# Two-level fast matrix products on one Trainium2 core: four PSUM banks for the forks, and another order of products and evictions in the steady unit

## Chip, cores and metric

The kernel runs on one core of one Trainium2 chip. The metric is the device time of one execution in microseconds (us), lower is better.

## The reference

A cross network of six layers on 16384 rows of 1024 columns in bfloat16:

```python
x = x0
for l in range(6):
    proj = jnp.einsum('bd,de->be', x, ws[l]) + bs[l]
    x = x0 * proj + x
```

## The kernel before

The kernel takes 1024 rows at a time through the six layers. One layer of one such block is a **unit**, and there are 96. A product of 2 by 2 blocks is made with seven products instead of eight (P1 to P7). In a **steady unit** (89 of 96) two of the seven, P5 and P2, are again made of seven inner products each (`5p1` to `5p7`, `2p1` to `2p7`). An outer product has four column blocks m = 0 to 3, each four matmuls of 128x128 by 128x512; an inner product is four matmuls with 256 columns.

PSUM has eight banks here: `pA[0..3]` for the outer sums, `pX[0..3]` for inner products and forks. A **fork** is a ScalarE copy of a sum from one bank to another, so that the sum goes on in both. F.m copies P1+P6 from `pA[m]` to a `pX` bank, where P3 is added; P7 and P4 go on in `pA[m]`:

```python
for m in range(KH):
    xb = m if one else m % 2
    group(f"P6.{m}", "6", pA[m], A[m], T[2], ["T2", A[m]], m, False)
    copy(f"F.{m}", pX[xb][:], pA[m][:], [A[m]], [Xn[xb]])
    group(f"P3.{m}", "3", pX[xb], Xn[xb], B22, [XI[1, 1], Xn[xb]], m, False)
    biased(f"E3.{m}", U[:, m, :], pX[xb][:], 0, m, [Xn[xb]], [f"U.{m}"])
    group(f"P7.{m}", "7", pA[m], A[m], T[3], ["T3", A[m]], m, False)
    ...
```

The inner products have forks of their own. This is the part that the argument touches (X is 5 with banks a, b = 0, 1, or 2 with banks 2, 3):

```python
inner(6, a, False)
copy(X + "f2", pX[b][:], pX[a][:], [Xn[a]], [Xn[b]])      # 2f2
inner(3, b, False)
copy(X + "e_c12", iu[X][:, 0], v3(b), [Xn[b]], [X + "u0"])
inner(7, a, False)                                        # 2p7 waits for 2f2
copy(X + "e_u3", iu[X][:, 1], v3(a), [Xn[a]], [X + "u1"])
inner(4, a, False)
copy(X + "e_c21", c(1, 0), v3(a), [Xn[a]], cn(1, 0))
ttop(X + "cc", ...)                                       # VectorE, needs both iu halves
```

`E1.m`, `E3.m` and so on are ScalarE evictions. VectorE makes the differences T1 to T4 that feed P5, P6, P7 and P4, and the layer's update. Five of its steps come up below: `5cc` and `2cc` add up inner results that ScalarE has put into `iu`, Q1 needs all of product 2's results, `2e_c21` among them, Qa ends that part of the update, and Ua needs the evictions E3. Each operation has a rank ("name@time"), and every engine's order is by rank, data allowing. `R2` is the table for all steady units but the first two, 87 units.

Of the kernel before, what the change touches and what calls it, by code (L numbers as in the profile page):

```python
# [24 lines left out]

R2 = ranks("""
P1.0@0 P1.2@0.86 5p5@1.73 5p1@2.16 P1.3@2.6 2p1@3.46 5p2@3.9 5p6@4.34 2p5@4.78 P1.1@5.21 5p7@6.08 5p3@6.51 2p2@6.95
2p6@7.39 5p4@7.82 P6.0@8.26 P6.1@9.13 2p7@9.99 2p3@10.43 P3.0@10.86 2p4@11.73 P6.2@12.16 P3.1@13.03 P6.3@13.89
P3.2@14.75 P3.3@15.62 P7.1@16.48 P7.0@17.34 P7.2@18.21 P7.3@19.07 P4.1@19.93 P4.0@20.8 P4.2@21.66 P4.3@22.52
E1.0@1.07 5e_p5@2.38 5f1@3.03 E1.2@3.48 5e_c11@4.55 5f2@5.2 2e_p5@5.65 2f1@6.3 5e_u3@6.75 E1.3@7.23 E1.1@7.8  # L30
2e_c11@8.37 5e_c21@8.85 2f2@9.33 F.0@9.78 5e_c12@10.23 2e_u3@10.71 2e_c12@11.18 F.1@11.66 E3.0@12.11 2e_c21@12.68
F.2@13.23 E3.1@14.1 F.3@14.96 E3.2@15.82 E3.3@16.69 E7.0@18.41 E7.1@18.98 E7.2@19.55 E7.3@20.14 E4.0@21.87 E4.1@22.44
E4.2@23.01 E4.3@23.59
T1@-1.14 5t13@0.59 5t2@3.06 2t13@3.39 5t4@5.13 2t2@6.6 T2@6.93 2t4@8.07 T4@8.4 5cc@10.88 T3@11.48 2cc@12.61 Q1@13.35
Qm@14.62 Qa@15.89 Ua@17.43 Um@18.7 Ux@19.97 Va@21.11 Wma@23.38 Wmb@24.58 Wx@25.31 Vm@27.38 Vx@28.85
""")
R0 = ranks("""
# [111 lines left out]
def kernel(  # L149
# [121 lines left out]
    for u, (pr, l) in enumerate(units):  # L271
        one, first, last = level1(u), u == 0, u == NU - 1
# [13 lines left out]
        def group(name, w, bank, bname, rhs, rname, m, start, u=u):  # L286
            def fn():
                for k in range(KH):
                    nc.tensor.matmul(bank[:], lhsT=wt[(u, w)][:, k, m * P:(m + 1) * P], rhs=rhs[:, k, :],  # L289
                                     start=(start and k == 0), stop=(k == KH - 1), skip_group_check=True)  # L290
            add(name, fn, rname + [f"w{u}.{w}" + ("a" if name in ("P5.0", "P5.1") and u == 0 else "")] if pr == 0 else rname, [bname], [w])

        def copy(name, dst, src, rd, wr):
            add(name, lambda: nc.scalar.copy(out=dst, in_=src), rd, wr)  # L294

        def biased(name, dst, src, eh, m, rd, wr, l=l):
            c = l * KD + eh * KH + m
            add(name, lambda: nc.scalar.activation(out=dst, in_=src, func=IDENT, bias=b_all[:, c:c + 1], scale=1.0), rd, wr)  # L298
# [52 lines left out]
        if first:  # L351

            for i, (d, n) in enumerate(TURNED):
                for k in range(KH):
                    xb = k if i < 2 else 2 + k % 2
# [75 lines left out]
                     ip5[X][:].unsqueeze(1).to_broadcast([P, 2, KQ, NQ]), ADD, [X + "u0", X + "u1", X + "ps"],  # L431
                     cn(0, 1) + cn(1, 1))
        for m in range(KH):
            xb = m if one else m % 2
            group(f"P6.{m}", "6", pA[m], A[m], T[2], ["T2", A[m]], m, False)
            copy(f"F.{m}", pX[xb][:], pA[m][:], [A[m]], [Xn[xb]])
            group(f"P3.{m}", "3", pX[xb], Xn[xb], B22, [XI[1, 1], Xn[xb]], m, False)
            biased(f"E3.{m}", U[:, m, :], pX[xb][:], 0, m, [Xn[xb]], [f"U.{m}"])
            group(f"P7.{m}", "7", pA[m], A[m], T[3], ["T3", A[m]], m, False)
            biased(f"E7.{m}", V[:, m, :], pA[m][:], 1, m, [A[m]], [f"V.{m}"])  # L440
            group(f"P4.{m}", "4", pA[m], A[m], T[4], ["T4", A[m]], m, False)
            if not (last and m == KH - 1):
                biased(f"E4.{m}", W[:, m, :], pA[m][:], 1, m, [A[m]], [f"W.{m}"])
# [201 lines left out]
```

## Time and profile before

| | before |
|---|---|
| median of 3 runs | 2277.09 us |
| span of the profiled run, granted clock | 2275.3 us, 0.999 |
| TensorE busy, matmul records | 2267.7 us, 12993 |
| VectorE, ScalarE busy | 92%, 81% |
| one steady unit, from recurring blocks | 23.45 us |

The lines behind these are in the prediction. The busy share of TensorE is no measure of holes below 0.16 us: a 512-column matmul is recorded as 379 ns, while the next one starts 216 ns later. So I use **starts**. A *hole* below is the time by which the start of the next matmul is later than 216 ns (512 columns) or 109 ns (256 columns) after the one before. "Holes in all" is the sum of those over 6 ns between 208 and 2200 us of a trace; for before it is 7.26 us.

### The profile page before, as it was taken

Reading aid. Unit: us, or ns where it says so; the run is one execution under the profiler, and the core shown is the slowest. Engines: PE = TensorE matmul, PEld = TensorE weight load, DVE = VectorE, ACT = ScalarE, POOL = GpSimd, SP = SyncE. Lnnn points to the kernel's source line nnn. Section 1 sums busy time; section 2 is a strip of 40 time slices with the busy share of each in tenths; the row PEclk is TensorE's granted clock in tenths of the full one; section 3 lists DMA queues with packets and bytes.
Section 4 is the critical chain, followed back from the end, with each engine's and each line's share of the span. In section 5 each row is a group of like instructions: output and inputs, shape, how many; then the busy total and the mean of one; then the engine's idle time right before and its main releaser. Section 6 shows DMA issues by size and latency. Waiting matters only on the chain.

```text
span 2275.3 us, 35076 instructions
## 1 busy us (share of the span) xinstructions
PE 2267.7 (100%) x12993; PEld 1266.7 (56%) x12993; DVE 2084.0 (92%) x2331; ACT 1844.5 (81%) x3234; POOL 24.5 (1%) x46
## 2 busy tenths in 40 slices
PE   9999999999999999999999999999999999999998
PEld 4455555555555555555555555555555555555554
DVE  8999999999999999999999999999999999989997
ACT  6678888888888888888888888888888888888887
POOL 1110000000000000000000000000000000000000
PEclk9999999999999999999999999999999999999999
DMA  8779797796977969779697796977969689696872
GB/s 280 231 269 297 252 249 262 221 297 210 246 264 222 286 216 255 257 220 286 213 269 247 227 283 205 283 235 227 286 200 286 232 230 286 196 291 227 234 248 66
DMA packets 620493, 557.03 MB, mean 245 GB/s; under 512 B 391456, under 2 KB 546592, under 8 KB 620320
## 3 DMA queue, kind: packets, MB, share of 16 engines
q1 hardware_dynamic: 614240, 534.58, 79.0%
q0 software_dynamic: 5488, 19.93, 2.3%
q8 instruction: 102, 1.67, 0.3%
q14 instruction: 71, 0.58, 0.1%
q10 hardware_dynamic: 592, 0.27, 0.0%
HBM read 437.79 MB, written 52.43 MB: 215 GB/s over the span
## 4 chain that ended last, share of the span: by engine, by line
PE 99%; DMA 0%; ACT 0%; DVE 0%; issue 0%
PE pA L289 58%; PE pX L411 24%; PE pX L289 17%; DMA ev<-in_x_dram 0%; PE pX L359 0%; PE pA L505 0%; PE pX L505 0%; DVE x0T L516 0%; ACT x0T L363 0%; ACT pX L294 0%; PE pA L366 0%
## 5 line engine op out<-in xcount | busy, mean ns | idle before, releaser
L289 PEld LDWEIGHTS <-wp 128*128 128x128 bf16 x7904 | 772.5, 98 | 839.5 <-issue 1.6
L289 PE MATMUL pA<-T,wp 128*128 128x512 bf16 x4608 | 1055.1, 379 | 0.0
L298 ACT ACTIVATE ev<-pA,b_all 128x512 bf16<-128x512 f32 x1123 | 705.0, 691 | 211.2 <-PE pA L289 210.8
L411 PEld LDWEIGHTS <-wp 128*128 128x128 bf16 x4984 | 487.0, 98 | 157.3 <-issue 15.4
L202 DVE TENSOR_TENSOR ev<-ev,x0T 128x2048 bf16<-128x2048 bf16 (+2 forms) x483 | 482.9, 1002 | 8.1 <-ACT ev L298 1.5
L202 DVE TENSOR_TENSOR xst<-ev,xst 128x2048 bf16<-128x2048 bf16 x319 | 389.1, 1220 | 19.1 <-DVE ev L202 0.9
L411 PE MATMUL pX<-ti,wp 128*128 128x256 bf16 x2848 | 397.6, 272 | 0.0
L202 DVE TENSOR_TENSOR ev<-ev,ev 128x2048 bf16<-128x2048 bf16 (+1 forms) x283 | 343.9, 1215 | 25.7 <-ACT ev L298 7.6
L289 PE MATMUL pX<-xst,wp 128*128 128x512 bf16 x1376 | 336.3, 379 | 0.0
L298 ACT ACTIVATE ev<-pX,b_all 128x512 bf16<-128x512 f32 x412 | 289.4, 706 | 56.1 <-PE pX L289 46.5
L289 PE MATMUL pA<-xst,wp 128*128 128x512 bf16 x1280 | 313.5, 379 | 0.0
L294 ACT COPY pX<-pA 128x512 f32<-128x512 f32 x412 | 256.2, 625 | 39.1 <-PE pA L289 38.4
L294 ACT CAST ev<-pX 128x512 bf16<-128x512 f32 x384 | 225.2, 620 | 47.8 <-ACT ev L298 37.3
L202 DVE TENSOR_TENSOR ev<-iu,ip 128x1024 bf16<-128x1024 bf16 x178 | 122.6, 689 | 121.1 <-ACT iu L294 121.1
L294 ACT COPY pX<-pX 128x512 f32<-128x512 f32 x356 | 208.7, 587 | 8.7 <-ACT ev L294 0.2
L294 ACT CAST iu<-pX 128x512 bf16<-128x512 f32 x356 | 197.0, 640 | 0.0
L202 DVE TENSOR_TENSOR T<-xst 128x2048 bf16<-128x2048 bf16 x160 | 194.9, 1218 | 0.3
L202 DVE TENSOR_TENSOR T<-xst,T 128x2048 bf16<-128x2048 bf16 x160 | 195.0, 1219 | 0.2
L411 PE MATMUL pX<-T,wp 128*128 128x256 bf16 x1068 | 160.2, 273 | 0.0
L294 ACT CAST ip<-pX 128x512 bf16<-128x512 f32 x178 | 104.8, 589 | 54.0 <-PE pX L411 54.0
L411 PE MATMUL pX<-xst,wp 128*128 128x256 bf16 x888 | 133.2, 273 | 0.0
L202 DVE TENSOR_TENSOR xst<-ev,x0T 128x2048 bf16<-128x2048 bf16 x64 | 78.3, 1223 | 1.6
(50 smaller groups left out, 641.0 us busy)
## 6 DMA issues: line engine op xcount, KB each, us to landing
wp<-Lc SPq DMA_DIRECT2D x538, 512.0 KB, 4.6
wp<-in_ws_dram SPq DMA_DIRECT2D x287, 512.0 KB, 5.4
out_dram<-x0T SPq DMA_DIRECT2D x30, 1024.0 KB, 8.7
Lc<-wp POOLq DMA_DIRECT2D x24, 512.0 KB, 5.9
Lc<-isum POOLq DMA_DIRECT2D x12, 512.0 KB, 6.7
w<-in_ws_dram SPq DMA_DIRECT2D x5, 512.0 KB, 6.3
ev<-in_x_dram SPq DMA_DIRECT2D x3, 512.0 KB, 7.0
out_dram<-x0T SPq DMA_DIRECT2D x3, 256.0 KB, 3.9
```

The source lines that it names most:

```text
L202: nc.vector.tensor_tensor(out=o, in0=a, in1=b, op=op)
L289: nc.tensor.matmul(bank[:], lhsT=wt[(u, w)][:, k, m * P:(m + 1) * P], rhs=rhs[:, k, :], start=(start and k == 0), stop=(k == KH - 1), skip ...
L294: add(name, lambda: nc.scalar.copy(out=dst, in_=src), rd, wr)
L298: add(name, lambda: nc.scalar.activation(out=dst, in_=src, func=IDENT, bias=b_all[:, c:c + 1], scale=1.0), rd, wr)
L411: nc.tensor.matmul(pX[bank][:, m * NQ:(m + 1) * NQ], lhsT=wv[:, k, m * P:(m + 1) * P], rhs=rhs[:, k, :], start=(start and m == 0 and k == ...
```

## The change

The intent: let P6 run ahead of P3 without sharing banks, and close waits in the steady unit. On TensorE P6.3 goes ahead of P3.1. On ScalarE 2e_c11 goes ahead of E1.1, 2f2 ahead of 5e_c21, 2e_c21 ahead of E3.0 and F.3 ahead of E3.1. On VectorE T3 goes ahead of 5cc. The order changes are in `R2` alone; the banks change in all 89 steady units.

```diff
-... P6.2@12.16 P3.1@13.03 P6.3@13.89
+... P6.2@12.16 P6.3@13.03 P3.1@13.89
-... E1.3@7.23 E1.1@7.8
-2e_c11@8.37 5e_c21@8.85 2f2@9.33 F.0@9.78 5e_c12@10.23 2e_u3@10.71 2e_c12@11.18 F.1@11.66 E3.0@12.11 2e_c21@12.68
-F.2@13.23 E3.1@14.1 F.3@14.96 E3.2@15.82 ...
+... E1.3@7.23 2e_c11@7.8 E1.1@8.28
+2f2@8.85 5e_c21@9.33 F.0@9.81 5e_c12@10.43 2e_u3@10.9 2e_c12@11.38 F.1@11.86 2e_c21@12.37 E3.0@12.85
+F.2@13.45 F.3@14.1 E3.1@14.96 E3.2@15.82 ...
-... T4@8.4 5cc@10.88 T3@11.48 2cc@12.61 ...
+... T4@8.4 T3@9.6 5cc@10.88 2cc@12.61 ...
@@
-            xb = m if one else m % 2
+            xb = m
```

More of the change, by code (lines that the diff above doesn't have):

```diff
@@ L27 @@
 P1.0@0 P1.2@0.86 5p5@1.73 5p1@2.16 P1.3@2.6 2p1@3.46 5p2@3.9 5p6@4.34 2p5@4.78 P1.1@5.21 5p7@6.08 5p3@6.51 2p2@6.95
-2p6@7.39 5p4@7.82 P6.0@8.26 P6.1@9.13 2p7@9.99 2p3@10.43 P3.0@10.86 2p4@11.73 P6.2@12.16 P3.1@13.03 P6.3@13.89
+2p6@7.39 5p4@7.82 P6.0@8.26 P6.1@9.13 2p7@9.99 2p3@10.43 P3.0@10.86 2p4@11.73 P6.2@12.16 P6.3@13.03 P3.1@13.89
 P3.2@14.75 P3.3@15.62 P7.1@16.48 P7.0@17.34 P7.2@18.21 P7.3@19.07 P4.1@19.93 P4.0@20.8 P4.2@21.66 P4.3@22.52
-E1.0@1.07 5e_p5@2.38 5f1@3.03 E1.2@3.48 5e_c11@4.55 5f2@5.2 2e_p5@5.65 2f1@6.3 5e_u3@6.75 E1.3@7.23 E1.1@7.8
-2e_c11@8.37 5e_c21@8.85 2f2@9.33 F.0@9.78 5e_c12@10.23 2e_u3@10.71 2e_c12@11.18 F.1@11.66 E3.0@12.11 2e_c21@12.68
-F.2@13.23 E3.1@14.1 F.3@14.96 E3.2@15.82 E3.3@16.69 E7.0@18.41 E7.1@18.98 E7.2@19.55 E7.3@20.14 E4.0@21.87 E4.1@22.44
+E1.0@1.07 5e_p5@2.38 5f1@3.03 E1.2@3.48 5e_c11@4.55 5f2@5.2 2e_p5@5.65 2f1@6.3 5e_u3@6.75 E1.3@7.23 2e_c11@7.8 E1.1@8.28
+2f2@8.85 5e_c21@9.33 F.0@9.81 5e_c12@10.43 2e_u3@10.9 2e_c12@11.38 F.1@11.86 2e_c21@12.37 E3.0@12.85
+F.2@13.45 F.3@14.1 E3.1@14.96 E3.2@15.82 E3.3@16.69 E7.0@18.41 E7.1@18.98 E7.2@19.55 E7.3@20.14 E4.0@21.87 E4.1@22.44
 E4.2@23.01 E4.3@23.59
-T1@-1.14 5t13@0.59 5t2@3.06 2t13@3.39 5t4@5.13 2t2@6.6 T2@6.93 2t4@8.07 T4@8.4 5cc@10.88 T3@11.48 2cc@12.61 Q1@13.35
+T1@-1.14 5t13@0.59 5t2@3.06 2t13@3.39 5t4@5.13 2t2@6.6 T2@6.93 2t4@8.07 T4@8.4 T3@9.6 5cc@10.88 2cc@12.61 Q1@13.35
 Qm@14.62 Qa@15.89 Ua@17.43 Um@18.7 Ux@19.97 Va@21.11 Wma@23.38 Wmb@24.58 Wx@25.31 Vm@27.38 Vx@28.85
```

## The prediction

> **What bounds the kernel now.** I read the page's busy shares first, then its chain that ended last.
>
> ```profile
> PE 2267.7 (100%) x12993; PEld 1266.7 (56%) x12993; DVE 2084.0 (92%) x2331; ACT 1844.5 (81%) x3234; POOL 24.5 (1%) x46
> ...
> PE 99%; DMA 0%; ACT 0%; DVE 0%; issue 0%
> ```
>
> TensorE is busy for the whole span and carries 99% of the chain. The page also gives it a full clock in all 40 slices. The other engines have slack, so the question is only whether TensorE's stream has holes, and the busy share cannot show small ones, because the ends of matmuls are modelled. So I read starts. One steady unit in the chain of waits, from one block of products 7 and 4 to the end of the next products 3:
>
> ```profile
> 1015.79 8.63 PE pA L289 x40
> 1024.42 0.87 PE pX L411 x8
> 1025.30 0.86 PE pA L289 x4
> 1026.16 1.75 PE pX L411 x16
> 1027.91 0.86 PE pA L289 x4
> 1028.77 2.18 PE pX L411 x20
> 1030.95 1.73 PE pA L289 x8
> ```
>
> 40 matmuls of 512 columns in 8.63 us are 215.75 ns each, and 20 of 256 columns in 2.18 us are 109 ns each. A steady unit has five outer products of 16 big matmuls (80) and two times seven inner products of 4 small ones (56): 80 x 0.21575 + 56 x 0.1092 = 17.26 + 6.12 = 23.38 us. The blocks of 40 recur at 992.34 and 1015.79 us in the same view, so a unit takes 23.45 us. Some 0.07 us of a unit is therefore not streaming. The timeline of all engines shows where:
>
> ```profile
> 1030.79 1.89 PE L289 MATMUL pA<-T,wp 128*128 128x512 bf16 x8
> ...
> 1030.95 1.09 ACT L294 CAST ev<-pX 128x512 bf16<-128x512 f32 x2
> 1031.89 0.64 ACT L294 COPY pX<-pX 128x512 f32<-128x512 f32 x1
> ...
> 1032.41 0.60 ACT L294 COPY pX<-pA 128x512 f32<-128x512 f32 x1
> 1032.58 0.60 PE L411 MATMUL pX<-ti,wp 128*128 128x256 bf16 x4
> 1032.58 0.75 PEld L411 LDWEIGHTS <-wp 128*128 128x128 bf16 x7 [0.18 <-issue]
> ```
>
> The first row is P6.0 and P6.1: eight matmuls should take 1.726 us, but the next product (2p7) starts 1.79 us later. The hole is 0.064 us (280 ns between two starts instead of 216 in the trace's own starts). 2p7 adds into pX[2], which the fork 2f2 (the COPY at 1031.89, ending 1032.53) reads; 2p7 starts 0.05 us after that end. So it waits for ScalarE, and the only place where the summary of waits hints at it is the weight loads' row:
>
> ```profile
> L411 PEld LDWEIGHTS <-wp 128*128 128x128 bf16 x4984 | 487.0, 98 | 157.3 <-issue 15.4
> ```
>
> Its "issue 15.4" is 84 pauses of 0.18 us, about one for each of the 87 units that use the changed ranks (96 units less 8 early ones and the last). A second, smaller hole is ahead of P3.3: P3.2 and P3.3 take 1.74 us from 1037.34 to 1039.08, 0.012 us over. P3.3 starts 0.05 us after F.3 (start 1037.60, 0.57 us) ends, and F.3 could only start when P6.3 was done.
>
> **What the skill says.** The Trainium skill, "TensorE: Matmul & The Clock Gate", section on 56 against 53.3 ns, gives N/2.4 GHz plus about 2.5 ns start to start at full clock: 215.7 ns at 512 columns. The trace agrees: 215.75. "Perfetto Trace Analysis", Tensor Engine Instruction, says the end of a matmul is estimated by the profiler; the trace agrees, as it hides the 64 ns hole in a row of busy time. "PSUM — Partial Sum Buffer", PSUM bank collisions, says two engines must not touch one bank at once and waits are to be set by bank; here both holes are a matmul waiting for a ScalarE copy on its bank. The same page, Engine vs sequencer instructions, calls ScalarE's queue strictly first in, first out: moving one eviction ahead delays the ones behind it, and the trace shows ScalarE working back to back from 1028.84 to 1036.5 us.
>
> **The change part by part.** No instruction is added or removed; only order and the banks of forks 2 and 3 change. All waits are reckoned from 2p2's neighbourhood, up to which neither engine's order changes. Durations and distances are from ScalarE's timeline: cast to next 0.475 us, biased eviction to next 0.575, copy to next 0.475 to 0.515; an operation on the bank that the one before it read starts 0.62 after it (5e_p5 at 1024.90, 5f1 at 1025.52); end to a waiting matmul 0.05.
>
> 1. 2e_c11 goes ahead of E1.1, and 2f2 ahead of 5e_c21. Old: E1.3 1029.80, E1.1, 2e_c11, 5e_c21, 2f2 1031.89. New: E1.3 1029.80, 2e_c11 1030.38, E1.1 1030.85, 2f2 1031.42. 2f2 is 0.47 us earlier, ends about 1032.06, and 2p7 is due without a hole at 1032.52: margin 0.4 us. **Gain 0.064 us a unit.**
>
> 2. What pays for it. E1.1 now ends 1031.55 and frees pA[1] at 1031.60; P6.1 is due at 1031.65: margin 0.05. 5e_c21 goes to 1031.93 and is directly followed by F.0 on its bank, so F.0 starts at 1032.58 (0.17 later), ends 1033.15, P3.0 is due at 1033.39: margin about 0.2. Then 5e_c12 1033.06, 2e_u3 1033.54, ending 1034.15 and releasing at 1034.20; 2p4 is due at 1034.26: margin 0.06. Two margins shrink to about 0.05 us; by the sum neither breaks.
>
> 3. P6.3 ahead of P3.1, with four banks. P6.3 now ends 0.86 us earlier; F.3 no longer shares a bank with E3.1 and starts about 1036.63, ending 1037.2, while P3.3 is due at 1038.14: margin 0.9 instead of -0.012. F.2 needs 2e_c21 (now ahead of E3.0, ending 1035.6) and starts near 1036.05 for P3.2 at 1037.27. **Gain 0.012 us a unit.**
>
> 4. T3 ahead of 5cc. VectorE idles 1.44 us at 5cc for ScalarE's iu. T3 (1.22 us) fills that, and Q1 comes some 0.45 us earlier. But Ua waits for E3.3, which is tied to P3.3, and from Ua on the row of VectorE is unchanged up to T2, which ends 1030.65 ahead of P6.0 at 1030.79. Gain on the path: none.
>
> Sum: 0.076 us a unit x 87 = 6.6 us. In the trace's starts, 81 holes of 64 ns and 87 of 12 ns are 6.2 us; a few irregular ones, around 1 us in all, I leave as they are. 2277.1 - 6.2 = 2270.9. I add 0.3 us for a margin that slips now and then: 2271.2.
>
> **Rivals.**
> First, the hole only moves: E1.1 to P6.1, or 2e_u3 to 2p4, becomes the new wait. For it: margins of 0.05 us, and ScalarE's durations spread (592 to 667 ns for iu). Against it: my sums leave both positive. A hole of 20 to 40 ns a unit gives back 2 to 3.5 us: 2273 to 2275.
> Second, ScalarE's later evictions or the new demand for pX[2] and pX[3] hold up products 3, and a unit gets longer than before. For it: forks 2 and 3 must now wait for the inner evictions. Against it: 2e_c21 and 2e_c12 end 0.4 us or more ahead of the forks. It would make 2278 or more.
> Third, weight transfers or the earlier T3 matter: nothing for it, since no TensorE wait on DMA shows in the steady part, and VectorE at 92% is not on the chain. 2277, or my number, unchanged.
>
> **Range and chances.** The floor is the stream without holes: 2277.1 - 6.6 - about 1 = 2269.5. Upwards I allow a new hole of about half the old one. Range 2269.7 to 2275.0. Even all holes together are 0.3% of the time, so faster by 2% is out of reach, and 2% slower would take 0.5 us of new waits a unit, which nothing points to.
>
> **What would show it.** Step 1: the weight loads' "issue" pauses of L411 vanish, and eight P6 matmuls to the next product take 1.73 us. Step 3: the blocks of products 7 and 4 recur every 23.37 to 23.39 us. Step 2: no new hole ahead of P6.1 or 2p4. Step 4: VectorE's idle time at iu falls from 121 us to under 75, with no change of its busy time. It is wrong if a unit still takes 23.43 us or more: then look at those two margins first.

## The result and the profile after

| | before | after |
|---|---|---|
| median of 6 runs | 2277.23 us | 2270.97 us (2270.48 to 2271.21) |
| ratio | | 0.9972, 95% interval 0.9959 to 0.9985 |
| unit, median of the trace's starts | 23.451 us | 23.380 us |
| holes in all | 7.26 us | 0.55 us |

A ratio is the mean time of one kernel's fast runs over that of the other's of the same rounds, so not quite the ratio of the medians. The change is 0.28% faster; its interval is clear of 1.

The page of the kernel after, busy times and the chain that ended last:

```profile
PE 2248.5 (99%) x12754; PEld 1267.4 (56%) x12993; DVE 2092.1 (92%) x2331; ACT 1847.8 (81%) x3234; POOL 24.5 (1%) x46
...
PE 99%; issue 1%; DMA 0%; ACT 0%; SPq 0%; DVE 0%; ACTq 0%
```

TensorE seems to have become idle for 1%, "issue". It has not: there are 12993 weight loads but 12754 matmul records, and each matmul has one weight load. 239 records are missing. The chain of waits of the kernel after shows how that looks:

```profile
1022.09 0.87 PE pX L411 x8
1022.96 0.86 PE pA L289 x4
1023.83 1.75 PE pX L411 x16
1025.57 0.05 issue
1025.62 0.81 PE pA L289 x3
1026.44 2.18 PE pX L411 x20
1028.62 1.73 PE pA L289 x8
1030.35 0.87 PE pX L411 x8
```

"issue" 0.05 and a group of 3 matmuls, 0.81, are together the 0.86 us of a group of four: one record of P1.1 is lost, not the time. I count a gap as a lost record where a weight load stands in it at its usual distance, and as a hole where the loads pause too. The last row is what answers to the prediction: in this stretch the two products behind P6 follow at once. The timeline of the same unit, all engines:

```profile
1028.46 1.89 PE L289 MATMUL pA<-T,wp 128*128 128x512 bf16 x8
1028.51 0.72 ACT L298 ACTIVATE ev<-pA,b_all 128x512 bf16<-128x512 f32 x1
...
1029.09 0.63 ACT L294 COPY pX<-pX 128x512 f32<-128x512 f32 x1
1029.61 0.63 ACT L294 CAST ev<-pX 128x512 bf16<-128x512 f32 x1
...
1030.18 0.60 PE L411 MATMUL pX<-ti,wp 128*128 128x256 bf16 x4
```

P6.0 and P6.1 now take 1030.18 - 1028.46 = 1.72 us until 2p7. The fork 2f2 (COPY) ends at 1029.72, 0.46 us ahead of 2p7. E1.1 (ACTIVATE) ends at 1029.23; P6.1, on the same bank, starts at 1028.46 + 0.863 = 1029.32. In the row of the weight loads the pauses are gone:

```profile
L411 PEld LDWEIGHTS <-wp 128*128 128x128 bf16 x4984 | 487.7, 98 | 151.5 <-issue 0.2
```

And the summary of waits shows where VectorE's idle time went, from 121.1 us at iu before to:

```profile
DVE ev L202 <- ACT iu L294: 60.7, 176, 0.7
...
DVE ev L202 <- ACT ev L298: 46.2, 94, 4.2
```

So the total came out as predicted. Whether each step did is for the experiments.

### The profile page after: what moved, and what is told of

It reads as the page before. It is cut to its first block, busy times and chain, and to the rows that moved or that the text cites. A ratio compares the mean times of both kernels' runs of the same rounds, so it can differ in the third digit from the quotient of the medians.

```text
span 2269.4 us, 34750 instructions
## 1 busy us (share of the span) xinstructions
PE 2248.5 (99%) x12754; PEld 1267.4 (56%) x12993; DVE 2092.1 (92%) x2331; ACT 1847.8 (81%) x3234; POOL 24.5 (1%) x46
## 3 DMA queue, kind: packets, MB, share of 16 engines
q8 instruction: 102, 1.67, 0.3%
## 4 chain that ended last, share of the span: by engine, by line
PE 99%; issue 1%; DMA 0%; ACT 0%; SPq 0%; DVE 0%; ACTq 0%
PE pA L289 58%; PE pX L411 24%; PE pX L289 17%; DMA ev<-in_x_dram 0%; ACT pX L294 0%; PE pA L505 0%; PE pX L359 0%; PE pX L505 0%; DVE x0T L516 0%; ACT ev L294 0%; ACT x0T L363 0%; ACT ip L294 0%; SPq L577 0%; SPq L574 0%; ACTq L294 0%
## 5 line engine op out<-in xcount | busy, mean ns | idle before, releaser
L289 PE MATMUL pA<-T,wp 128*128 128x512 bf16 x4468 | 1033.0, 379 | 7.3
L298 ACT ACTIVATE ev<-pA,b_all 128x512 bf16<-128x512 f32 x1123 | 717.5, 692 | 211.2 <-PE pA L289 164.0
L289 PE MATMUL pX<-xst,wp 128*128 128x512 bf16 x1371 | 323.3, 379 | 0.3
L289 PE MATMUL pA<-xst,wp 128*128 128x512 bf16 x1205 | 302.4, 379 | 3.9
L294 ACT CAST ev<-pX 128x512 bf16<-128x512 f32 x384 | 232.1, 606 | 47.9 <-ACT ev L298 37.4
L294 ACT COPY pX<-pA 128x512 f32<-128x512 f32 x412 | 237.5, 602 | 21.7 <-PE pA L289 18.7
L202 DVE TENSOR_TENSOR ev<-iu,ip 128x1024 bf16<-128x1024 bf16 x178 | 123.2, 692 | 60.7 <-ACT iu L294 60.7
```

What stands on the lines that cost most here:

```text
L202: nc.vector.tensor_tensor(out=o, in0=a, in1=b, op=op)
L289: nc.tensor.matmul(bank[:], lhsT=wt[(u, w)][:, k, m * P:(m + 1) * P], rhs=rhs[:, k, :], start=(start and k == 0), stop=(k == KH - 1), skip ...
L294: add(name, lambda: nc.scalar.copy(out=dst, in_=src), rd, wr)
L298: add(name, lambda: nc.scalar.activation(out=dst, in_=src, func=IDENT, bias=b_all[:, c:c + 1], scale=1.0), rd, wr)
```

## The experiments

"Before" beside a run is the kernel before, in the same rounds.

| run | median us | before beside it | ratio (95%) | holes in all, us |
|---|---|---|---|---|
| e1_scalar_only | 2272.0 | 2276.19 | 0.9982 (0.9969 to 0.9994) | 2.73 |
| e2_pe_and_banks_only | 2275.68 | 2276.19 | 0.9998 (0.9985 to 1.001) | 6.21 |
| e3_t3_only | 2276.58 | 2276.19 | 1.0001 (0.9988 to 1.0015) | 6.77 |
| e4_after_two_banks | 2329.56 | 2276.19 | 1.0234 (1.022 to 1.0248) | 56.8 |
| e5_E11_behind_2f2 | 2320.66 | 2276.79 | 1.0193 (1.0177 to 1.0209) | 48.8 |
| e6_after_T3_back | 2271.8 | 2276.79 | 0.9978 (0.9966 to 0.9991) | 1.67 |
| e7_banks_only | 2275.61 | 2276.79 | 0.9995 (0.9982 to 1.0007) | 5.82 |
| e8_E31_ahead_of_F3 | 2318.9 | 2276.79 | 1.0186 (1.0172 to 1.02) | 47.4 |
| e9_after_again | 2270.5 | 2276.49 | 0.9974 (0.9961 to 0.9986) | 0.56 |
| e10_after_T3_back_again | 2271.46 | 2276.49 | 0.9979 (0.9966 to 0.9991) | 1.72 |
| e11_scalar_and_T3 | 2272.49 | 2276.49 | 0.9982 (0.9969 to 0.9994) | 2.76 |
| e12_only_F3_shares | 2276.4 | 2276.49 | 0.9999 (0.9985 to 1.0013) | 6.57 |

All twelve gave correct results.

### e1: the early ScalarE move alone

```diff
-E1.3@7.23 E1.1@7.8
-2e_c11@8.37 5e_c21@8.85 2f2@9.33 F.0@9.78
+E1.3@7.23 2e_c11@7.8 E1.1@8.28
+2f2@8.85 5e_c21@9.33 F.0@9.78
```

> Kernel before with one move alone: 2e_c11 ahead of E1.1 and 2f2 ahead of 5e_c21 on ScalarE. Theory (the 64 ns hole ahead of 2p7 is a wait for 2f2, and this move alone closes it): unit 23.451 to 23.387 us, the weight loads' 84 pauses of 0.18 us gone, the 12 ns hole ahead of P3.3 stays; 2277.2 - 5.3 = 2271.9 us. Rival (the four banks or the T3 move gave the time): 2277.2, holes as before.

It came to 2272.0 us. No hole is left ahead of 2p7 and the weight loads' pauses fall to 0.5 us: the hole was a wait for 2f2, as predicted. But 5.4 us of holes closed there and the time fell by only 4.2. The starts show why: some 50 holes ahead of P6.0, mostly of about 10 ns and three of 220, and two of 0.13 us ahead of 2p1. Before had three of 160 to 184 ns at P6.0 and none of the small ones. P6.0 waits for T2 from VectorE. The prediction's sum had no such term.

### e2: the rest without the early ScalarE move and T3

```diff
 (kernel after)
-2e_c11@7.8 E1.1@8.28
-2f2@8.85 5e_c21@9.33 F.0@9.81
+E1.1@7.8
+2e_c11@8.37 5e_c21@8.85 2f2@9.33 F.0@9.81
-T3@9.6 5cc@10.88 2cc@12.61
+5cc@10.88 T3@11.48 2cc@12.61
```

> Kernel after with the early ScalarE moves (E1.1, 2e_c11, 5e_c21, 2f2) and T3 put back as before; the four banks, P6.3 ahead of P3.1 and F.3 ahead of E3.1 stay. Theory: the 64 ns hole ahead of 2p7 is back, the 12 ns hole ahead of P3.3 is gone; unit 23.44, 2277.2 - 1.1 = 2276.1 us. Rival (the banks carry the gain): 2271.

The pauses of the weight loads are back (here the same row of this run), the holes ahead of P3.3 are gone, and the unit is 23.442 us as expected:

```profile
L411 PEld LDWEIGHTS <-wp 128*128 128x128 bf16 x4984 | 487.2, 98 | 157.2 <-issue 15.6
```

The time, 0.5 us under before, is not told from zero; the trace's holes fell by 1.05 us.

### e3 and e7: T3 alone, banks alone

```diff
 e3 (kernel before)
-T4@8.4 5cc@10.88 T3@11.48 2cc@12.61
+T4@8.4 T3@9.6 5cc@10.88 2cc@12.61
 e7 (kernel before)
-            xb = m if one else m % 2
+            xb = m
```

> Kernel before with T3 moved ahead of 5cc on VectorE alone. Theory: off the path, VectorE's idle time at iu falls from 121 us to under 75 and appears instead at Ua; unit 23.45, 2277.2 us. Rival (VectorE at 92% also paces): 2275 or less.

> Kernel before with the forks on four banks and no order changed. Theory: F.3 waits for P6.3's end, not for the bank, so nothing moves: the holes of 64 and 12 ns stay, 2277.2 us (within 0.5). Rival (the bank of E3.1 held up F.3): the 12 ns hole closes, 2276.1.

T3 alone did nothing to the time (2276.58 against 2276.19). VectorE's wait at iu fell to 46.5 us; what it saved came back not at Ua, as I expected, but as 76.6 us of waiting for an eviction into `ev`, which by its place in VectorE's row is Q1 waiting for 2e_c21.

Banks alone is a miss. I expected nothing, but all the 12 ns holes ahead of P3.3 are gone, which is the rival's outcome. ScalarE's timeline around F.3, kernel before:

```profile
1036.68 0.69 ACT L298 ACTIVATE ev<-pX,b_all 128x512 bf16<-128x512 f32 x1
1037.60 0.57 ACT L294 COPY pX<-pA 128x512 f32<-128x512 f32 x1 [0.23 <-PE pA L289]
1038.41 0.69 ACT L298 ACTIVATE ev<-pX,b_all 128x512 bf16<-128x512 f32 x1 [0.24 <-PE pX L289]
```

and with four banks alone:

```profile
1036.06 0.69 ACT L298 ACTIVATE ev<-pX,b_all 128x512 bf16<-128x512 f32 x1
1036.92 0.57 ACT L294 COPY pX<-pA 128x512 f32<-128x512 f32 x1 [0.18 <-PE pA L289]
1037.78 0.69 ACT L298 ACTIVATE ev<-pX,b_all 128x512 bf16<-128x512 f32 x1 [0.29 <-PE pX L289]
```

The rows are E3.1, F.3 and E3.2. E3.1 had ended at 1037.37 in the kernel before, 0.23 us ahead of F.3, so its result was not what F.3 waited for. Yet with four banks F.3 is 0.86 us ahead of E3.2 instead of 0.81, 0.05 us earlier. Measured from the start of P6.3's last matmul, F.3 starts 471 ns later in the kernel before and 416 ns later with four banks (medians). In the compiled order F.3 had two waits, one for TensorE and one for ScalarE's own E3.1, and the raw trace has a semaphore instruction at 1037.540, F.3 starting 57 ns after it. With four banks F.3 has the wait for TensorE alone, and no such instruction stands before it.

### e12: only F.3 shares a bank

```diff
 (kernel before)
-            xb = m if one else m % 2
+            xb = m if one else (0, 1, 2, 1)[m]
```

> Kernel before with fork 2 on pX[2] but fork 3 on pX[1], so that F.3 alone shares a bank with E3.1. Theory (F.3 starts about 0.055 us later when it must wait for ScalarE's own E3.1 as well as for TensorE, though E3.1 has long ended): the 12 ns hole ahead of P3.3 is as before, F.3 comes 0.81 us ahead of E3.2 and not 0.86; 2276.5 or so, no faster than 0.6 us under before. Rival (F.2's bank made the hole): the hole is gone, 1.2 us under before.

The 12 to 14 ns holes ahead of P3.3 are back in 85 units, F.3 is again 0.81 us ahead of E3.2 (1037.35 and 1038.16) and 471 ns behind the start of P6.3's last matmul, with the semaphore instruction in front of it, and the time is that of before. So it is F.3's second wait that made this hole. That the extra instruction, and not something else about a second wait, costs the 0.05 us was not tested by itself.

### e4 and e8: what the banks and F.3's place are worth to the new order

```diff
 e4 (kernel after)
-            xb = m
+            xb = m if one else m % 2
 e8 (kernel after)
-F.3@14.1 E3.1@14.96
+E3.1@14.1 F.3@14.96
```

> Kernel after with the forks back on two banks (m mod 2), all orders as after where the data allow. Theory (four banks are what lets P6.3 and F.3 run ahead): F.3 must wait until E3.1 has read pX[1], E3.1 until P3.1 ends; F.3 then ends about 0.6 us past the time P3.3 is due, so a hole of 0.5 to 0.7 us ahead of P3.3 in each of 87 units: 2271 + 45 to 60 = 2316 to 2331 us. Rival (banks are incidental, order counts): within 2 us of 2271.

> Kernel after (four banks, P6.3 ahead of P3.1) with ScalarE's E3.1 put back ahead of F.3. Theory: E3.1 waits for P3.1's end and holds F.3 up in ScalarE's queue; F.3 starts 0.57 us after E3.1, P3.3 waits 0.5 to 0.57 us a unit: 2271 + 43 to 50 = 2314 to 2321 us, a little less than with two banks, where F.3 also waits for E3.1 to end. Rival (only the bank ties F.3 to E3.1): 2271.

Both came out as expected: 2329.56 and 2318.9 us, with one hole ahead of P3.3 in nearly every unit, 0.678 us (e4) and 0.564 us (e8). Here, for e4, TensorE's timeline and then ScalarE's:

```profile
1033.39 1.89 PE L289 MATMUL pX<-x0T,wp 128*128 128x512 bf16 x8
1035.80 1.02 PE L289 MATMUL pX<-x0T,wp 128*128 128x512 bf16 x4 [0.52 <-ACT pX L294]
```

```profile
1034.46 0.69 ACT L298 ACTIVATE ev<-pX,b_all 128x512 bf16<-128x512 f32 x1 [0.65 <-PE pX L289]
1035.17 0.57 ACT L294 COPY pX<-pA 128x512 f32<-128x512 f32 x1
```

E3.1 starts when P3.1 is done; F.3 follows when E3.1 has ended (1035.15), ends at 1035.74, and P3.3 starts at 1035.80. The new order of products is thus only harmless with four banks and with F.3 ahead of E3.1. The page says 0.52 us idle where the starts say 0.678: the modelled ends hide 0.16 us of every hole.

### e5: the narrow margin

```diff
 (kernel after)
-2e_c11@7.8 E1.1@8.28
-2f2@8.85
+2e_c11@7.8 2f2@8.28
+E1.1@8.85
```

> Kernel after with E1.1 one place later on ScalarE, behind 2f2. It tests the narrow margin: in the kernel after, E1.1 ends about 0.08 us ahead of P6.1, which writes its bank. Theory: 2f2 now waits 0.62 us for 2e_c11 (same bank), E1.1 ends about 1.05 us after 2e_c11 started plus 0.7, so P6.1 waits 0.5 to 0.6 us a unit: 2271 + 43 to 52 = 2314 to 2323 us, with a hole between P6.0 and P6.1. Rival (the bank of P1.1 is free long before, my margin is wrong): 2271.

2320.66 us, a hole of 0.576 us between P6.0 and P6.1 in nearly every unit. TensorE and then ScalarE:

```profile
1024.61 1.03 PE L289 MATMUL pA<-T,wp 128*128 128x512 bf16 x4
1026.05 1.02 PE L289 MATMUL pA<-T,wp 128*128 128x512 bf16 x4 [0.41 <-ACT ev L298]
```

```profile
1025.31 0.69 ACT L298 ACTIVATE ev<-pA,b_all 128x512 bf16<-128x512 f32 x1
```

E1.1 ends at 1026.00 and P6.1 starts 0.05 us later. The margin that the change left there is real and only some 0.04 us wide.

### e6, e9, e10, e11: what T3 is worth once the big hole is closed

```diff
 e6 and e10 (kernel after)
-T3@9.6 5cc@10.88 2cc@12.61
+5cc@10.88 T3@11.48 2cc@12.61
 e11 (kernel before): the moves of e1 and of e3 together
 e9: the kernel after, unchanged
```

> Kernel after with T3 put back behind 5cc. Theory: T3's place is off the path also without the holes; VectorE's idle time at iu rises from 61 us to about 120 or more, 2271.0 us (within 0.5). Rival (with the holes closed VectorE is the next limit and needs the T3 move): 2272 or more, new holes ahead of P6.0 or P7.

e6 came to 2271.8, outside the 0.5 us that I had allowed, and its trace had the same small holes ahead of P6.0 as e1. That favoured the rival. As the two kernels had not run beside each other, I repeated the pair together, with e11 beside it:

> The kernel after itself, as the measure for the runs beside it. 2271.0 us, about 0.6 us of holes in the steady part.

> Kernel after with T3 put back behind 5cc, once more beside the kernel after. New theory: with the hole ahead of 2p7 closed and T3 late, VectorE's row reaches T2 too late by some 8 ns, so P6.0 waits in about half the units, and by 0.2 us in two or three; 0.6 to 1.2 us slower than the kernel after beside it. Rival (the 0.8 us between the first two runs was chance): equal within 0.3 us.

> Kernel before with the early ScalarE move and the T3 move, two banks and P3 order as before. New theory: the holes ahead of P6.0 that the ScalarE move alone had are gone, the 12 ns ahead of P3.3 stay (1.1 us in 87 units); 1.0 us slower than the kernel after beside it, about 2272.0. Rival (T3 is nothing): the holes ahead of P6.0 are as with the ScalarE move alone, and it is 2 us slower than the kernel after.

The kernel after took 2270.19 to 2270.91 us and the one with T3 put back 2271.32 to 2272.34 on the same chip: no overlap, 1.0 us between the medians, and 1.16 us between their holes. Its holes ahead of P6.0 are some 35 of about 10 ns, three of 24 to 36 and three of 219 to 226; two of 0.13 us are ahead of 2p1. T3 does count here. VectorE's timeline with T3 put back, from Q1 to Ua (columns: start, duration, and in brackets idle time before):

```profile
1033.90 1.23 DVE L202 TENSOR_TENSOR ev<-ev,ev 128x2048 bf16<-128x2048 bf16 x1
1035.16 1.22 DVE L202 TENSOR_TENSOR ev<-ev,x0T 128x2048 bf16<-128x2048 bf16 x1
1036.49 1.23 DVE L202 TENSOR_TENSOR xst<-ev,xst 128x2048 bf16<-128x2048 bf16 x1
1037.63 1.22 DVE L202 TENSOR_TENSOR ev<-ev,ev 128x2048 bf16<-128x2048 bf16 x1
```

and of the kernel after beside it:

```profile
1033.18 1.22 DVE L202 TENSOR_TENSOR ev<-ev,ev 128x2048 bf16<-128x2048 bf16 x1 [0.30 <-ACT ev L294]
1034.44 1.23 DVE L202 TENSOR_TENSOR ev<-ev,x0T 128x2048 bf16<-128x2048 bf16 x1
1035.77 1.22 DVE L202 TENSOR_TENSOR xst<-ev,xst 128x2048 bf16<-128x2048 bf16 x1
1037.43 1.23 DVE L202 TENSOR_TENSOR ev<-ev,ev 128x2048 bf16<-128x2048 bf16 x1 [0.44 <-ACT ev L298]
```

The last row of each is Ua. In the kernel after it waits 0.44 us for E3.3, so VectorE has time to spare. With T3 put back it does not wait there at all: from 5cc up to T2 VectorE's own row sets the time. And the row starts late, because 5cc waits for 5e_c12 in `iu`. Here is 5cc in the kernel before and with T3 put back:

```profile
1033.56 0.69 DVE L202 TENSOR_TENSOR ev<-iu,ip 128x1024 bf16<-128x1024 bf16 x1 [1.44 <-ACT iu L294]
1031.37 0.69 DVE L202 TENSOR_TENSOR ev<-iu,ip 128x1024 bf16<-128x1024 bf16 x1 [1.59 <-ACT iu L294]
```

From T2's end to P6.0's start there are 52 to 54 ns in most units of e10, e1 and e11, which is the latency of a wait that binds, and 77 to 79 ns (medians) in before, after and e9. So the kernel before had only some 24 ns to spare at T2, and another 0.16 us at Ua, where it waited for E3.3. Two things used these up, by medians of the starts: 5cc comes 0.14 us later after P6.0's start (2.769 us before, 2.910 in e1, 2.908 in e10), because the early moves push 5e_c12 back on ScalarE, and the unit is 0.06 to 0.07 us shorter. In three units the kernel before was late too: its holes of 160 to 184 ns at P6.0 end 53 ns after T2. In two of them Qa comes 0.35 us late, in one Vx 0.2 us; what these waited for was not traced.

e11 missed, and its rival came out, 2.0 us slower than the kernel after: it has T3 early, and still some 35 holes of about 10 ns and three of 0.22 us ahead of P6.0, as e1 has. Its Q1 waits 0.88 us for 2e_c21, which in e11 still stands behind E3.0 on ScalarE; in the kernel after 2e_c21 is ahead of E3.0 and Q1 waits 0.30 us. So the four cases are complete, all with the early ScalarE move: neither (e1), 2e_c21 early alone (e10), T3 early alone (e11), both (the kernel after). Only with both are the small holes gone. The cases are not quite pure: e1 and e11 also have two banks and the old order of P3.1 and P6.3.

## Why the prediction was right, and where its steps were not

- **The bound and the floor.** Right. The unit fell to 23.380 us, the predicted floor of 23.37 to 23.39, and 2270.97 us stands against 2271.2.
- **Step 1, 2f2 earlier, 0.064 us a unit.** Right in mechanism and size of the hole (e1, e2). Worth alone it was 4.2 us and not the 5.3 that e1 expected, because of VectorE (step 4).
- **Step 2, margins of 0.05, 0.2 and 0.06 us hold.** Right: no new hole at P6.1, P3.0 or 2p4; less the 0.05 us of latency the starts leave 0.036, 0.17 and 0.04 us (medians), and e5 shows the first margin to be real. But the step delayed 5e_c12 by 0.18 us in its own sum and did not carry that on to 5cc, which waits for it.
- **Step 3, P6.3 early with four banks, 0.012 us a unit.** The size is right (e7: 1.2 us less time; the holes ahead of P3.3, 1.05 us in all, are gone). The reason is not: the prediction said "F.3 could only start when P6.3 was done", but the banks alone close the hole (e7), since F.3 then has one wait fewer and starts 0.05 us earlier after the same P6.3. The new order gives P3.3 a wide margin that nothing was seen to need, and is harmful without banks and F.3's place (e4, e8).
- **Step 4, T3, "Gain on the path: none".** This is the step that failed. It is none on the kernel before (e3), but about 1.0 us on the kernel after (e9, e10), together with 2e_c21's place (e11), which the prediction looked at only as a risk. The error has two parts. I read one unit: T2's end at 1030.65 against P6.0 at 1030.79, 0.14 us, but that unit is one of the one in six with 0.145 us; an ordinary unit has 0.077, of which 0.053 is the latency, so 0.024 us are left. And I took Ua to be "tied to P3.3": it was, but by 0.16 us only, and the later 5cc (0.14 us) and the shorter unit (0.07 us) together take more than the two margins.
- **The third rival, "the earlier T3 matter: nothing for it".** Wrong for the same reason: with T3 late, VectorE, idle for 8% of the span but at other places, came some 10 ns too late for TensorE without holes.
- **The sum** was right because the parts were changed together: T3 and 2e_c21 pay for the VectorE holes that the early 2f2 exposes. That was luck as far as the prediction goes: it gave neither of the two a gain. The parts do not add: e1, e7 and e3 taken alone give about 4.2 + 1.2 + 0 = 5.4 us, the whole 6.0 to 6.3. Some 0.3 us of the holes that closed were at P6.0, among the irregular ones that the prediction left as they are.
- **VectorE's idle time** at iu fell to 60.7 us, under the 75 predicted. Its busy time rose from 2084.0 to 2092.1 us, where no change was predicted. It does no more work: the durations of its records add up to 2214.1 and 2214.9 us, and only the time in which two records overlap fell, from 130.1 to 122.8 us.

Left open: the 0.55 us of irregular holes that the kernel after still has; what makes T2 late by 0.2 us in single units; and whether P6.3 ahead of P3.1 is needed at all, since banks, both ScalarE moves and T3 without it were not run. No version was found that beats the kernel after, and with 0.55 us of holes the steady part has little left to gain by order.

## What to carry to other kernels

When the bound engine reads 100% busy, measure its recurring block against the number of instructions in it times their start-to-start time; the difference is all that reordering can win. Then ask which engine has the next longest row, because closing the holes takes slack from it too, and follow every operation that the change delays to whoever waits for it on another engine: a move that is worth nothing alone can be what makes the other move pay. And read a margin in several units, not in one, when the program has kinds of units.

## What the Trainium skill lacked or had wrong

- "TensorE: Matmul & The Clock Gate", Back-to-back issue gap, calls N/2.4 + 2.5 ns the isolated gap and gives 131 ns per 512-column matmul for streams of weight load and matmul. Here every matmul has its own weight load, and the stream ran at 215.75 ns (512 columns) and 109 ns (256), which is the formula and not the stream figure.
- "Perfetto Trace Analysis", Identifying Dependency Chains, says that an instruction waiting on multiple engines may have a semaphore instruction inserted before it, but gives no cost. Here a ScalarE copy with a second, long satisfied wait started about 0.05 us later (57 ns after that instruction; F.3 0.81 instead of 0.86 us ahead of E3.2).
- "Perfetto Trace Analysis", Tensor Engine Instruction, says that a matmul's end is estimated, but not what that hides: here 0.16 us of every hole, so that a 0.678 us hole shows as 0.52 and one of 0.064 us as none.
- No page was found on lost matmul records: 239 of 12993 are missing in eight of the twelve experiments' traces and in that of the kernel after, at the same places of a unit, and the chain then shows 0.05 us of "issue" there.
